# One layer-2 step in split halves, one step placed ahead of the next block, and residual additions by transfers, in an attention, LayerNorm, MLP and gate kernel

## The chip, the core and the metric

The kernel runs on one core of a Trainium2 chip. Its engines each run their own queue of instructions in a fixed order: TensorE (PE) multiplies matrices into PSUM, ScalarE (ACT), VectorE (DVE) and GpSimd (POOL) work elementwise, SyncE (SP) issues most transfers (DMAs). An engine that needs what another makes waits on a semaphore, and what stands behind the waiting instruction in its queue waits too. The metric is the device time of one execution in microseconds, as a median of several runs; lower is better.

## The reference

Three stages follow one another: a mutual attention between 8 batches of 512 tokens and 32 state tokens, a normalised MLP with a residual, and a gated output. Cut to what is computed:

```python
scores = scale * x @ state.T            # per batch and head, 8 heads of 64
xread = softmax(scores) @ state         # [8, 8, 512, 64]
sread = softmax(scale * state @ x.T) @ x  # [8, 8, 32, 64]
x = concat([xread, sread], axis=2)      # -> [8, 576, 512]
xn = (x - mean) / sqrt(var + 1e-6) * g_ln
x = x + relu(xn @ w_ch1) @ w_ch2        # 512 -> 2048 -> 512
gate = sigmoid(causal_conv5(x, conv_w))
out = (gate * (x @ w_val)) @ w_out
```

## The kernel before

**Work and its tiles.** The tokens are cut into nine blocks: b = 0 to 7 are the 512 tokens of one batch each, block 8 holds the 256 state tokens. Everything lies with the model or hidden columns on the 128 partitions and the tokens along the free side, so one matmul is 128x128 by 128x512. `segment(b, f0, f1, ...)` runs the MLP of a block in steps f = 0 to 15 of 128 hidden columns. A step has three parts: layer 1 puts h into a PSUM tile (two buffers, named mm in the trace); the evacuation makes hid from it; layer 2 (`second`) adds hid times a slice of w2 to four PSUM accumulators, acc0 to acc3. Layer 2 of a step is put off by one: `run_pending` writes it behind the layer 1 of the next step, so the evacuation of h runs beside matmuls.

**Two kinds of products.** Most products are in split halves: a value is kept as a high and a low half in the fast float format, and `mm3` (L77 to L80) does three matmuls for one product. Block 0's steps 0 to 3 (`plain`, QF = 4) use plain float matmuls, in layer 1 (L729) and in layer 2 (L785); a plain matmul needs the high part alone. A step in split halves has six layer-1 matmuls (L734) and twelve for layer 2. For it ScalarE makes the high half of hid with a Relu (L763) and VectorE the low half (L770); both read h. Weights come in 512 KB loads; ScalarE (L573, L575) and VectorE (L581, L583, L585, custom instructions) decode them, and for split steps ScalarE makes the high half (L653, or L631 for those that were first used plain) and VectorE the low one (L654, L634). The slots of this decode are handed out by `weights`.

**Blocks 0 and 1 are interleaved:** steps 0 to 7 of block 0, steps 0 to 7 of block 1, steps 8 to 15 of block 0, steps 8 to 15 of block 1; then blocks 2 to 7, block 8, and the value, gate and output stage. At the end of each of these half passes `second` scales each accumulator by the row of 1/std on VectorE (L799, into a t tile) and adds it to the block's residual x (L802). After a block's last step x goes to DRAM (x2d) and its last four columns are copied (the halo) for the convolution.

**m groups.** The first layer's weights are combined with the attention's state beforehand: `m_group` (L147) multiplies them into two PSUM tiles, `m_evac` (L158) scales and shifts them into mb, and `split_sb` (L73, L74) splits mb in halves of m. A group m (b, q) feeds four steps of layer 1. The groups for (0, 1) and (1, 0) are made in the middle of block 0's first pass. Group (0, 1) takes its two PSUM tiles from the mm buffers of h, group (1, 0) from the at buffers, in which the attention scores of block 1 stand before. The scores are centred and squared around L474, L476, L478 and L482 (LayerNorm of the attention's result), their row maxima are the reduces of L284, and ScalarE's exp (L286) reads them.

**What sets the order.** PE's order is the order in which the code is written. The orders of ACT, DVE, POOL and SP come from a scheduler that goes by priorities: `at_prio` sets one, HLEAD = 4000 puts work on PE's path ahead, DLEAD = 3000 the decode, and `behind` ties an instruction behind a marked one.

## Time and profile before

| | us |
|---|---|
| median of 3 runs (870.91 to 871.29) | 871.06 |
| the profiled execution, in all | 870.83 |
| its span in the trace | 868.9 |
| PE busy | 862.1 |
| DVE busy | 587.7 |
| ACT busy | 369.7 |
| POOL busy | 199.4 |

The span is what the trace shows from the first to the last instruction; about 2 us lie around it. Busy times are those of the profiled execution. In the page's groups PE's largest lines are the three products of layer 2 (L78 to L80, 560 each, 211 to 213 us) and layer 1 (L734, 744, 194.2 us). PE's total of waits is read in the view of waits, and what the other engines do beside it in the timelines, where each row gives its start from the span's start, its length and, in brackets, the idle time ahead of it and what ended it.

### The profile page before, as it was taken

How to read it: one execution, taken by the hardware profiler on the slowest of the kernel's cores; microseconds unless marked ns; L12 is line 12 of the kernel's file. 1: busy time of each engine (PE TensorE's matmuls, PEld its weight loads, DVE VectorE, ACT ScalarE, POOL GpSimd, SP SyncE). 2: the span in 40 equal slices, each digit the busy share in tenths (PEclk: the TensorE clock that was granted, in tenths of full speed). 3: DMA queues.
4: the chain of work that ended last, by engine and by line, in shares of the span. 5: the costliest groups of instructions: out<-in, count | busy, mean ns of one | idle time of the engine just before them, and what ended most of it. 6: DMA issues, size and time to landing. Idle time of an engine off the chain costs nothing.

```text
span 868.9 us, 12589 instructions
## 1 busy us (share of the span) xinstructions
PE 862.1 (99%) x4941; PEld 661.2 (76%) x4942; DVE 587.7 (68%) x995; ACT 369.7 (43%) x696; POOL 199.4 (23%) x162
## 2 busy tenths in 40 slices
PE   9999999999999999999999999999999999999998
PEld 3367767677777777778777777777899888888886
DVE  6999983874746754563674566353389799988870
ACT  5965942233333332432332343132256465455432
POOL 0020200013135133312513422252201223322100
PEclk9999999999999999999999999999999999999999
DMA  9925200321312221230231103010140212223212
GB/s 360 406 85 154 95 29 0 123 79 51 100 53 77 81 72 42 69 99 19 76 98 52 49 11 67 1 49 1 51 144 2 98 73 97 73 98 97 91 55 73
DMA packets 35643, 72.80 MB, mean 84 GB/s; under 512 B 11904, under 2 KB 20608, under 8 KB 31488
## 3 DMA queue, kind: packets, MB, share of 16 engines
q1 hardware_dynamic: 34816, 71.60, 23.9%
q8 instruction: 39, 0.64, 0.3%
q10 hardware_dynamic: 768, 0.40, 0.2%
q14 instruction: 20, 0.16, 0.1%
HBM read 51.01 MB, written 20.97 MB: 83 GB/s over the span
## 4 chain that ended last, share of the span: by engine, by line
PE 86%; DVE 3%; ACT 1%; DMA 0%; issue 0%; DVEq 0%; ACTq 0%
PE mm L734 18%; PE acc L78 16%; PE acc L79 16%; PE acc L80 16%; PE mm L80 2%; PE mm L78 2%; PE mm L79 2%; PE at L80 2%; PE at L78 2%; PE at L79 2%; PE at L147 2%; PE mm L147 1%; PE at L337 1%; PE acc L397 1%; DVE mb L158 1%; PE at L221 1%
## 5 line engine op out<-in xcount | busy, mean ns | idle before, releaser
L78 PE MATMUL acc<-hid,w 128*128 128x512 f32 (+1 forms) x560 | 212.6, 380 | 0.4 <-DVE x L402 0.2
L79 PE MATMUL acc<-hid,w 128*128 128x512 f32 (+1 forms) x560 | 211.4, 378 | 0.0
L80 PE MATMUL acc<-hid,w 128*128 128x512 f32 (+1 forms) x560 | 211.4, 378 | 0.0
L770 DVE SCALAR_TENSOR_TENSOR hid<-mm,hid 128x512 fp32r<-128x512 f32 (+1 forms) x140 | 91.6, 654 | 156.5 <-ACT hid L763 156.3
L734 PE MATMUL mm<-ahl,m 128*128 128x512 f32 x744 | 194.2, 396 | 0.5
L763 ACT ACTIVATE hid<-mm 128x512 fp32r<-128x512 f32 (+2 forms) x144 | 82.3, 571 | 215.5 <-PE mm L734 196.4
L734 PEld LDWEIGHTS mm<-ahl,m 128*128 128x128 f32 x744 | 137.0, 188 | 47.6 <-DVE mb L158 9.3
L78 PEld LDWEIGHTS acc<-hid,w 128*128 128x128 f32 x560 | 105.3, 188 | 24.7 <-issue 1.7
L80 PEld LDWEIGHTS acc<-hid,w 128*128 128x128 f32 x560 | 105.4, 188 | 20.0
L79 PEld LDWEIGHTS acc<-hid,w 128*128 128x128 f32 x560 | 105.4, 188 | 19.1
L861 DVE SCALAR_TENSOR_TENSOR ahl<-big,cw,ahl 128x511 f32<-128x511 f32 (+3 forms) x128 | 102.1, 843 | 0.3
L74 POOL TENSOR_TENSOR m<-mb,m 128x512 fp32r<-128x512 f32 x50 | 65.0, 1320 | 111.1 <-ACT m L73 111.0
L73 ACT ACTIVATE m<-mb 128x512 fp32r<-128x512 f32 x62 | 39.0, 632 | 80.8 <-DVE mb L158 80.5
L847 POOL TENSOR_TENSOR w<-big,w 128x512 fp32r<-128x512 f32 x24 | 37.9, 1611 | 93.0 <-ACT w L845 93.0
L79 PE MATMUL acc<-w,raw 128*128 128x512 f32 (+1 forms) x144 | 54.3, 377 | 0.0
L80 PE MATMUL acc<-w,raw 128*128 128x512 f32 (+1 forms) x144 | 54.3, 377 | 0.0
L78 PE MATMUL acc<-w,raw 128*128 128x512 f32 (+1 forms) x144 | 54.3, 377 | 0.0
L387 POOL TENSOR_TENSOR rstd<-rstd,nhalf 128x16 f32<-128x16 f32 (+1 forms) x9 | 25.7, 2854 | 114.3 <-DVE rstd L385 114.2
L799 DVE TENSOR_TENSOR t<-acc,t 128x512 f32<-128x512 f32 (+1 forms) x44 | 27.8, 660 | 24.3 <-PE acc L80 24.3
L802 POOL TENSOR_TENSOR x<-t,x 128x512 f32<-128x512 f32 x20 | 25.1, 1287 | 78.7 <-DVE t L799 78.7
L873 ACT ACTIVATE ahl<-ahl 128x512 f32<-128x512 f32 (+1 forms) x36 | 21.6, 608 | 45.6 <-DVE ahl L861 45.3
L902 DVE TENSOR_TENSOR w<-ahl,w 128x512 fp32r<-128x512 f32 (+1 forms) x36 | 30.7, 859 | 13.0 <-ACT w L901 12.8
(202 smaller groups left out, 1258.8 us busy)
## 6 DMA issues: line engine op xcount, KB each, us to landing
w<-in_w SPq DMA_DIRECT2D x20, 512.0 KB, 8.0
big<-in_xT SPq DMA_DIRECT2D x8, 1024.0 KB, 4.9
big<-in_xk SPq DMA_DIRECT2D x8, 1024.0 KB, 5.2
x2d<-x SPq DMA_DIRECT2D x8, 1024.0 KB, 4.2
big<-x2d SPq DMA_DIRECT2D x8, 1024.0 KB, 4.8
out<-hid SPq DMA_DIRECT2D x16, 512.0 KB, 2.8
raw<-in_w SPq DMA_DIRECT2D x12, 512.0 KB, 5.6
a2d<-t SPq DMA_DIRECT2D x48, 64.0 KB, 1.7
```

What stands on the lines that cost most here:

```text
L73: a = nc.scalar.activation(hi, src, AF.Copy)
L74: eng.tensor_tensor(lo, src, hi.bitcast(F32), op=ALU.subtract)
L78: nc.tensor.matmul(acc, lhsT=wh, rhs=xl, start=first, stop=False)
L79: nc.tensor.matmul(acc, lhsT=wl, rhs=xh, start=False, stop=False)
L80: nc.tensor.matmul(acc, lhsT=wh, rhs=xh, start=False, stop=last)
L734: nc.tensor.matmul(h, lhsT=m[:, u, w, cols], rhs=ahls[b][:, u, x], start=(i, u) == (0, 0), stop=(i, u) == (2, 1),)
L763: a = nc.scalar.activation(hid[:, 0], h, AF.Relu)
L770: marks["dve"] = nc.vector.scalar_tensor_tensor(hid[:, 1], h, 0.0, hid[:, 0].bitcast(F32), op0=ALU.max, op1=ALU.subtract)
L799: marks["dve"] = nc.vector.tensor_tensor(t, accs[d], rrow, op=ALU.mult)
L847: nc.gpsimd.tensor_tensor(lo, src, hi.bitcast(F32), op=ALU.subtract)
L861: t = nc.vector.scalar_tensor_tensor(g[:, j:], x[:, :n - j], cw_sb[:, k, PAD - j:TAPS - j], g[:, j:], op0=ALU.mult, op1=ALU.add)
L902: a = nc.vector.tensor_tensor(hl[:, 1], gt[:, e], hl[:, 0].bitcast(F32), op=ALU.subtract)
```

## The change

Four things are changed. Line numbers behind the change are larger by 4 to 14 (L147 is then L151, L463 and L459 of before are L467 and L463, L78 to L80 are L81, L734 is L747, L763 is L777, L770 is L784, L785 is L799, L799 is L813, L585 is L589).

1. Step 3 of block 0 does its layer 2 in split halves (`plain_out`): twelve matmuls of L81 in place of four plain ones, the high by high product first. VectorE makes a low half of its hid (L784), and w2_3 is split right after its decode (`split_last`, L73 and L74), where before it was split later with the other three.
2. Block 0's eighth step (f = 7) writes its layer 2 ahead of block 1's first layer 1 (`run_pending` at (1, 0, 0)), where before it stood behind it.
3. For group (0, 1) the m group, its sum and its evacuation are written ahead of `weights`, where before `weights` came first; the low halves of some w2 splits are tied behind the group's low half.
4. In the four half passes of blocks 0 and 1, the sixteen additions of VectorE at L802 become sixteen transfers that POOL issues and that add t to x where it lies (L817, 128x512, 256 KB each). L813 writes t tiles from the same six buffers as before, and the x2d store and the halo copy read the same x.

```diff
+    def mm3(acc, wh, wl, xh, xl, first, last, low_last=False):
+        terms = [(wh, xl), (wl, xh), (wh, xh)]
+        if low_last:
+            terms.reverse()
+        for i, (w, x) in enumerate(terms):
+            nc.tensor.matmul(acc, lhsT=w, rhs=x, start=first and i == 0, stop=last and i == 2)
...
+    def plain_out(b, f):
+        return b == 0 and f < QF - 1
...
-            return lambda: decode_a(r, c), add, lambda: None
+
+            def split_last():
+                w2s[j] = hl = sb([P, 2, DM], F32R, f"w2_{j}")
+                split_sb(hl[:, 0], hl[:, 1], c, nc.vector)
+
+            return lambda: decode_a(r, c), add, split_last if j == QF - 1 else lambda: None
...
             if j < QF + 2:
                 behind(hi, "parts")
+                behind(lo, "group_low")
...
+            if (b, f, f0) == (1, 0, 0):
+                at_prio(base + 200)
+                run_pending()
             at_prio(base)
             h = ps(ps_mm, "mm", [P, n])
...
                     colsum_parts(1)
+                    m_group(*unit, "mm")
+                    colsum(1)
+                    m_evac(*unit)
                     weights(base)
                     at_prio(base - 1500)
-                    m_group(*unit, "mm")
-                    colsum(1)
                 else:
                     m_group(*unit)
-                m_evac(*unit)
+                    m_evac(*unit)
...
-            if not plain(b, f):
+            if not plain_out(b, f):
                 marks["dve"] = nc.vector.scalar_tensor_tensor(
...
-                        eng.tensor_tensor(dst, grouped(b, t), grouped(b, x1[:, d, :]), op=ALU.add)
+                        if b < 2:
+                            nc.gpsimd.dma_start(out=dst, in_=t, accum_op=ALU.add)
+                        else:
+                            eng.tensor_tensor(dst, grouped(b, t), grouped(b, x1[:, d, :]), op=ALU.add)
...
-    order = order[:12] + [("s", j) for j in range(QF)] + order[12:]
+    order = order[:12] + [("s", j) for j in range(QF - 1)] + order[12:]
```

**At the m group (0, 1).** PE before, from layer 1 of step 3 (mm_415) over the colsum matmuls to the two halves of the group (mm_443, mm_444), with the engines that each instruction waits for:

```order
L729 MATMUL mm_415<-aT_288,m_307 128x512 x2
L182 MATMUL at_418<-w_2_70_330,g_82 32x512 [waits DVE_49,Activation_49]
L182 MATMUL at_418<-w_2_70_330,g_82 32x512 [waits DVE_49]
L182 MATMUL at_418<-w_3_88_390,g_82 32x512 [waits DVE_49] x2
L147 MATMUL mm_443<-w_2_70_330,stg_224 32x512 [waits Activation_49]
L147 MATMUL mm_443<-w_2_70_330,stg_224 32x512
L147 MATMUL mm_443<-w_3_88_390,stg_224 32x512 x2
L147 MATMUL mm_444<-w_2_70_330,stg_224 32x512 [waits Activation_49]
```

PE after, the same place (mm_418 is step 3's h, mm_428 and mm_429 the group's halves):

```order
L742 MATMUL mm_418<-aT_288,m_307 128x512 x2
L186 MATMUL at_421<-w_2_70_330,g_82 32x512 [waits DVE_49,Activation_49]
L186 MATMUL at_421<-w_2_70_330,g_82 32x512 [waits DVE_49]
L186 MATMUL at_421<-w_3_88_390,g_82 32x512 [waits DVE_49] x2
L151 MATMUL mm_428<-w_2_70_330,stg_224 32x512 [waits Activation_49]
L151 MATMUL mm_428<-w_2_70_330,stg_224 32x512
L151 MATMUL mm_428<-w_3_88_390,stg_224 32x512 x2
L151 MATMUL mm_429<-w_2_70_330,stg_224 32x512 [waits DVE_49]
```

The rows stand in the same order, but the group's second half, which takes the buffer of step 3's h, waits for Activation before and for DVE now. DVE before, from the decode of w2_3 (w_14_76) on (c_425 and c_434 are w2_4 and w2_5):

```order
L585 ISA w_14_76_350<-w_3_24_123,w_14_76_350 128x1024
L581 TENSOR_SCALAR w_3_88_390<-w_3_88_390 128x512
L583 TENSOR_SCALAR w_3_88_390<-w_3_88_390 128x512
L585 ISA w_3_88_390<-w_13_25_125,w_3_88_390 128x1024
L581 TENSOR_SCALAR c_425<-c_425 128x512
L263 TENSOR_TENSOR ahl_471<-aT_288,ahl_471 128x512 x2
L581 TENSOR_SCALAR c_434<-c_434 128x512
L583 TENSOR_SCALAR c_425<-c_425 128x512
L583 TENSOR_SCALAR c_434<-c_434 128x512
L585 ISA c_425<-w_4_28_131,c_425 128x1024
L585 ISA c_434<-w_5_29_133,c_434 128x1024
L654 TENSOR_TENSOR w_4_95_426<-c_425,w_4_95_426 128x512
```

DVE after, from the decode of w2_3 on (c_450 and c_459 are w2_4 and w2_5, hid_468 is step 3's hid):

```order
L589 ISA w_14_76_350<-w_3_24_123,w_14_76_350 128x1024
L74 TENSOR_TENSOR w_3_89_401<-w_14_76_350,w_3_89_401 128x512
L585 TENSOR_SCALAR w_3_88_390<-w_3_88_390 128x512
L587 TENSOR_SCALAR w_3_88_390<-w_3_88_390 128x512
L589 ISA w_3_88_390<-w_13_25_125,w_3_88_390 128x1024
L585 TENSOR_SCALAR c_450<-c_450 128x512
L267 TENSOR_TENSOR ahl_475<-aT_288,ahl_475 128x512 x2
L585 TENSOR_SCALAR c_459<-c_459 128x512
L587 TENSOR_SCALAR c_450<-c_450 128x512
L587 TENSOR_SCALAR c_459<-c_459 128x512
L589 ISA c_450<-w_4_28_131,c_450 128x1024
L784 SCALAR_TENSOR_TENSOR hid_468<-mm_418,hid_468 128x512
```

The low half of w2_3 (L74 w_3) is new behind its decode, and step 3's low half (L784 hid_468) stands between the two decodes of w2_4 and w2_5.

**Between the centring and the score maxima.** DVE before, from the last L474 to the two maxima of block 1's scores (at_534, at_535):

```order
L474 TENSOR_TENSOR t_110_493<-x_73_341,at_476 128x512
L585 ISA c_511<-w_7_31_137,c_511 128x1024
L654 TENSOR_TENSOR w_6_114_503<-c_502,w_6_114_503 128x512
L770 SCALAR_TENSOR_TENSOR hid_527<-mm_520,hid_527 128x512
L478 TENSOR_TENSOR t_107_483<-t_107_483,t_108_486 128x512
L478 TENSOR_TENSOR t_109_490<-t_109_490,t_110_493 128x512
L654 TENSOR_TENSOR w_7_116_512<-c_511,w_7_116_512 128x512
L482 TENSOR_TENSOR t_107_483<-t_107_483,t_109_490 128x512
L225 STREAM_TRANSPOSE t_121_544<-at_534 128x512
L225 STREAM_TRANSPOSE t_122_546<-at_535 128x512
L284 TENSOR_REDUCE nmax_550<-at_534 128x1
L284 TENSOR_REDUCE nmax_550<-at_535 128x1
```

DVE after, from the first step behind the four centrings (L478) on:

```order
L585 TENSOR_SCALAR c_506<-c_506 128x512
L585 TENSOR_SCALAR c_515<-c_515 128x512
L784 SCALAR_TENSOR_TENSOR hid_531<-mm_524,hid_531 128x512
L482 TENSOR_TENSOR t_108_487<-t_108_487,t_109_490 128x512
L587 TENSOR_SCALAR c_506<-c_506 128x512
L587 TENSOR_SCALAR c_515<-c_515 128x512
L482 TENSOR_TENSOR t_110_494<-t_110_494,t_111_497 128x512
L589 ISA c_506<-w_6_30_135,c_506 128x1024
L589 ISA c_515<-w_7_31_137,c_515 128x1024
L486 TENSOR_TENSOR t_108_487<-t_108_487,t_110_494 128x512
L663 TENSOR_TENSOR w_6_115_507<-c_506,w_6_115_507 128x512
L663 TENSOR_TENSOR w_7_117_516<-c_515,w_7_117_516 128x512
```

Behind these follow L784 hid_584, the two transposes and the two maxima (L288). The four tensor_scalars and one more decode of w2_6 and w2_7 (c_506, c_515) now stand in this piece, and a second low half of hid.

**At the end of block 0's first pass.** PE before, from layer 1 of (1, 0) (mm_742) to the first two of step 7's twelve (hid_675):

```order
L734 MATMUL mm_742<-ahl_641,m_614 128x512 [waits Activation_49] x2
L734 MATMUL mm_742<-ahl_641,m_614 128x512 [waits Pool_49] x2
L734 MATMUL mm_742<-ahl_641,m_614 128x512 [waits DVE_49] x2
L78 MATMUL acc_79_366<-hid_675,w_7_116_512 128x512
L79 MATMUL acc_79_366<-hid_675,w_7_116_512 128x512
```

Ten more of the twelve follow. PE before, from the last of them to the two tiles of L459 (mm_779 and mm_780, the state's product for block 1):

```order
L80 MATMUL acc_82_372<-hid_675,w_7_116_512 128x512
L459 MATMUL mm_779<-aT_638,sn_raw_113 64x512 [waits DMAHW4_49]
L459 MATMUL mm_779<-aT_638,sn_raw_113 64x512
L459 MATMUL mm_780<-aT_638,sn_raw_113 64x512 [waits DVE_49]
L459 MATMUL mm_780<-aT_638,sn_raw_113 64x512
```

The second tile waits for DVE's reading of mm_742, which has had the twelve matmuls to end.
PE after, from the last of step 7 on (mm_780 is now layer 1 of (1, 0), mm_791 and mm_792 the two tiles of L463):

```order
L81 MATMUL acc_82_372<-hid_687,w_7_117_516 128x512 x3
L747 MATMUL mm_780<-ahl_653,m_626 128x512 [waits Activation_49] x2
L747 MATMUL mm_780<-ahl_653,m_626 128x512 [waits Pool_49] x2
L747 MATMUL mm_780<-ahl_653,m_626 128x512 [waits DVE_49] x2
L463 MATMUL mm_791<-aT_650,sn_raw_113 64x512 [waits DMAHW4_49]
L463 MATMUL mm_791<-aT_650,sn_raw_113 64x512
L463 MATMUL mm_792<-aT_650,sn_raw_113 64x512 [waits DVE_49]
L463 MATMUL mm_792<-aT_650,sn_raw_113 64x512
```

Layer 1 of (1, 0) now stands directly ahead of L463, and the second tile's first matmul takes the buffer that DVE's low half of (1, 0) must have read; before, step 7's twelve matmuls stood between the two.

## Rows read from the trace of the kernel before

**Rows 1.** The page: busy us of each engine; PE's granted clock by slice.

```profile
PE 862.1 (99%) x4941; PEld 661.2 (76%) x4942; DVE 587.7 (68%) x995; ACT 369.7 (43%) x696; POOL 199.4 (23%) x162
...
PEclk9999999999999999999999999999999999999999
```

**Rows 2.** PE's waits: engine, line, releaser; us in total, times, longest.

```profile
PE mm L1095 <- DVE m L1090: 1.3, 1, 1.3
PE acc L221 <- DMA big<-in_xT: 0.6, 1, 0.6
PE acc L169 <- ACT cs L211: 0.2, 1, 0.2
PE acc L78 <- DVE x L402: 0.2, 1, 0.2
```

**Rows 3.** PE's timeline: start, us, engine, line, operation, tiles, count, idle time before.

```profile
39.14 1.09 PE L147 MATMUL mm<-w,stg 64*32 64x512 f32 x16
...
45.95 1.55 PE L734 MATMUL mm<-ahl,m 128*128 128x512 f32 x6
47.34 3.60 PE L785 MATMUL acc<-hid,w 128*128 128x512 f32 x8
50.86 1.09 PE L221 MATMUL at<-big,st_raw 64*32 64x512 f32 x16
...
53.37 0.39 PE L78 MATMUL acc<-hid,w 128*128 128x512 f32 x1
...
56.09 1.52 PE L734 MATMUL mm<-ahl,m 128*128 128x512 f32 x6
57.55 1.09 PE L147 MATMUL at<-w,stg 64*32 64x512 f32 x16
...
68.01 1.65 PE L734 MATMUL mm<-ahl,m 128*128 128x512 f32 x6
69.50 0.39 PE L78 MATMUL acc<-hid,w 128*128 128x512 f32 x1
...
72.31 1.09 PE L459 MATMUL mm<-aT,sn_raw 32*64 32x512 f32 x8
...
197.45 0.50 PE L78 MATMUL acc<-hid,w 128*128 128x512 f32 x1 [0.18 <-DVE x L402]
```

**Rows 4.** ACT's timeline, 33 to 70 us.

```profile
33.70 0.62 ACT L763 ACTIVATE hid<-mm 128x512 f32<-128x512 f32 x1
34.19 0.69 ACT L573 ACTIVATE w<-w 128x512 f32<-128x512 f32 x1
...
56.13 0.69 ACT L286 ACTIVATE t<-at,nmax 128x512 f32<-128x512 f32 x1
...
69.76 0.60 ACT L763 ACTIVATE hid<-mm 128x512 fp32r<-128x512 f32 x1 [1.09 <-PE mm L734]
```

**Rows 5.** DVE's timeline, 33 to 56 us.

```profile
33.83 0.69 DVE L585 CUSTOM_DVE_ANT_0 w<-w,w 128x1024 uint16<-128x1024 uint16 x1
34.91 0.43 DVE L581 TENSOR_SCALAR w<-w 128x512 f32<-128x512 f32 x1 [0.40 <-ACT w L573]
...
39.08 1.28 DVE L585 CUSTOM_DVE_ANT_0 c<-w,c 128x1024 uint16<-128x1024 uint16 x2
...
46.41 2.47 DVE L474 TENSOR_TENSOR t<-x,at 128x512 f32<-128x512 f32 x4
...
53.02 1.30 DVE L225 STREAM_TRANSPOSE t<-at 128x512 f32<-128x512 f32 x2
54.25 1.25 DVE L284 TENSOR_REDUCE nmax<-at 128x1 f32<-128x512 f32 x2
```

**Rows 6.** Transfers by kind: issuing queue, count, KB each, median us to landing.

```profile
raw<-in_w SPq DMA_DIRECT2D x12, 512.0 KB, 5.6
...
t<-a2d SPq DMA_DIRECT2D x12, 256.0 KB, 2.7
...
x1d<-t SPq DMA_DIRECT2D x32, 16.0 KB, 3.8
```

More of the change, by code (lines that the diff above doesn't have):

```diff
@@ L73, in split_sb @@
         a = nc.scalar.activation(hi, src, AF.Copy)
-        eng.tensor_tensor(lo, src, hi.bitcast(F32), op=ALU.subtract)
-        return a
-    def mm3(acc, wh, wl, xh, xl, first, last):
-        nc.tensor.matmul(acc, lhsT=wh, rhs=xl, start=first, stop=False)
-        nc.tensor.matmul(acc, lhsT=wl, rhs=xh, start=False, stop=False)
-        nc.tensor.matmul(acc, lhsT=wh, rhs=xh, start=False, stop=last)
+        return a, eng.tensor_tensor(lo, src, hi.bitcast(F32), op=ALU.subtract)
+    def mm3(acc, wh, wl, xh, xl, first, last, low_last=False):
[4 more added lines that the diff above has]
+            nc.tensor.matmul(acc, lhsT=w, rhs=x, start=first and i == 0, stop=last and i == 2)
     def at_prio(p):
@@ L162, in m_evac @@
             if not plain(b, 4 * q):
-                marks["group"] = split_sb(m[:, u, 0], m[:, u, 1], mb, nc.vector if b < 2 and (b, q) != (1, 0) else nc.gpsimd)
+                marks["group"], marks["group_low"] = split_sb(m[:, u, 0], m[:, u, 1], mb, nc.vector if b < 2 and (b, q) != (1, 0) else nc.gpsimd)
     def m_first(diag):
@@ L653, in split @@
             hi = nc.scalar.activation(hl[:, 0], c, AF.Copy)
-            nc.vector.tensor_tensor(hl[:, 1], c, hl[:, 0].bitcast(F32), op=ALU.subtract)
+            lo = nc.vector.tensor_tensor(hl[:, 1], c, hl[:, 0].bitcast(F32), op=ALU.subtract)
             if j < QF + 2:
                 behind(hi, "parts")
+                behind(lo, "group_low")
         mark = "group" if j == QF + 3 else "act"
@@ L761, in segment @@
             at_prio(base - HLEAD)
-            hid = sb([P, 2, n], F32 if plain(b, f) else F32R, "hid")
+            hid = sb([P, 2, n], F32 if plain_out(b, f) else F32R, "hid")
             a = nc.scalar.activation(hid[:, 0], h, AF.Relu)
@@ L783, in second @@
                     cols = slice(d * P, (d + 1) * P)
-                    if plain(b, f):
+                    if plain_out(b, f):
                         nc.tensor.matmul(accs[d], lhsT=plain_w2[f][:, cols], rhs=hid[:, 0], start=f == f0, stop=f == f1 - 1)
                     else:
-                        mm3(accs[d], w2s[f][:, 0, cols], w2s[f][:, 1, cols], hid[:, 0], hid[:, 1], f == f0, f == f1 - 1)
+                        mm3(accs[d], w2s[f][:, 0, cols], w2s[f][:, 1, cols], hid[:, 0], hid[:, 1], f == f0, f == f1 - 1, (b, f) == (0, QF - 1))
                     if f == f1 - 1:
```

## The prediction

> **What bounds the kernel now.** I read the page's busy shares first [rows 1]. TensorE (PE) is busy 862.1 of 868.9 us, and its granted clock shows 9, the top digit, in every slice, so it runs at its upper level, 2.4 GHz, from start to end. Its own waits come next [rows 2]: 1.3 us at the start, then 0.6, 0.2 and 0.2. So the time is PE's queue of matmuls almost without a gap. A matmul that goes away is worth its length, and a wait that the change opens on PE is added in full. The question is therefore not what VectorE (DVE) is spared, but whether PE, in its fixed order, now comes to places where the other engines are late. For that I read the first 80 us of PE, ScalarE (ACT) and DVE side by side [rows 3 to 5]: there DVE works almost back to back while PE never waits.
>
> Neighbouring instructions overlap a little in the timeline, so I count from start to start. Four of DVE's L474 take 2.47 us together where one shows some 0.68, so one costs 0.60 and the overlap is 0.08; a tensor_scalar of 0.43 costs 0.34 [rows 5].
>
> **Part 1, step 3 of block 0 in split halves: -0.8 us.** Before, the layer 2 of step 3 is the eight passes of L785 from 47.34 to 50.86, 3.52 us; a step in split halves is the twelve of L78 to L80 from 53.37 to 56.09, 2.72 us [rows 3]. The difference, 0.80 us, is PE work that is gone. Both stretches stand without waits, so I take it whole.
>
> **Part 1 also adds work ahead of step 3: a wait at the m group (0,1), +2.2 us.** ScalarE and VectorE now split w2_3 before block 0's step 2 is evacuated, and VectorE owes a low half of step 3's hid. PE's second half of the m group at L147 takes the PSUM buffer of step 3's h; before it waited for ACT's evacuation alone, now for DVE's low half (the order of PE below the change shows the wait turn from Activation to DVE). On DVE that low half stands behind the first of the two c decodes. Step by step:
> - Before, ACT starts to evacuate step 2 at 33.70, at once behind L463 [rows 4]. Now the high half of w2_3 stands between, and it needs DVE's L585 of that weight, which runs from 33.83 to 34.52 [rows 5]. So it starts near 34.6, takes 0.55 to its successor, as L573 at 34.19 does, and the evacuation starts at 35.15 instead of 33.70: ACT is 1.45 later.
> - ACT's next, L573 at 34.19, feeds DVE's L581 at 34.91, on which DVE already waited 0.40 [rows 5]. Now it starts at 36.36; DVE's new 0.60 (the low half of w2_3) falls into that wait.
> - From 34.91 to the end of the first c decode (the second of L585 starts 39.08 + 0.60 = 39.68) DVE has 4.77 us of back-to-back work [rows 5]: 41.13. The low half takes 0.68: 41.81; with 0.1 for the signal PE goes on at 41.9.
> - Without a wait PE would start that half at 39.14 plus half of L147's 1.09 less the overlap, 0.51: 39.65 [rows 3]. Wait: 2.2.
>
> The bounds: if ACT's delay were swallowed and only DVE's own 0.60 counted, the half would start at 41.05, a wait of 1.4; with a few signals of 0.1 more on the way, 2.4. I take 2.2, since the 0.40 of waiting on ACT shows that DVE stands on ACT's rhythm there.
>
> **The new order of `weights` and m_group: a wait at the m group (1,0), +2.2 us.** The mb and m halves now go ahead of the weights, and the four decode steps of w2_6 and w2_7 stand behind the four L474. Count DVE from the first L474 to the end of the second score reduce (L284). Before: 46.41 to 54.25 + 1.25 = 55.50, 9.1 us, of which 48.81 (46.41 + 4 times 0.60) to 53.02, 4.2 us, is other work between L474 and the transposes [rows 5]. Now that other work is nine full instructions and four tensor_scalars, 6.8 us. In all, seventeen of 0.60 and four of 0.34: 11.6 us. ACT's exps follow. In before, the second starts 56.13 and ends 56.82, when PE comes to L147 at 57.55 [rows 3, 4]: 0.73 us of cover. From PE's L734 of (0,4), at 45.95, DVE's first L474 stands 0.46 later. The reduces therefore end 12.1 after that mark, and the second exp some 1.6 later (two short nmax, two exps), at 13.7. PE's way from the mark is 1.39 + 2.72 (step 3, now split) + 2.51 + 2.72 + 1.46 = 10.80 to L147, and 0.51 more to its second half, which takes the second score's buffer: 11.3, with a margin for a signal 11.4 [rows 3]. So 2.2 to 2.3; I take 2.2. Two causes add: 2.5 from DVE and 0.8 that PE is now faster, less the cover of 0.73 and some 0.3 of rounding. Bounds: 1.5, if DVE's delay after the first wait leaves it ahead of PE by the 0.46 and the exps pipeline with the reduces as before; 2.6, if each step carries its signal.
>
> **Part 2, step 7's layer 2 ahead of block 1's first layer 1: +1.2 us.** It adds no instruction. Before, PE ran L734 of (1,0) from 68.01, then the twelve of step 7 from 69.50, then L459 at 72.31 [rows 3]: the 2.72 us of step 7 hid the evacuation of (1,0). Now L734 of (1,0) is followed at once by L459, whose second half takes the buffer of (1,0)'s h and waits for DVE's low half. Evacuation by the rows: matmuls end at 69.50, ACT starts 69.76 and ends 70.36 [rows 4], DVE's low half 0.68 and a signal 0.1: 1.7 us after the end of layer 1. The first half of L459 covers 0.5 of it. Wait: 1.2; bounds 1.1 and 1.8 (if one DVE instruction of 0.6 is in its way). What the move gives in return, an earlier end of block 0's accumulators, PE does not wait for here [rows 2].
>
> **Part 3, residual additions by transfers: -0.3 us.** Sixteen DVE additions of 0.60, 9.6 us of DVE, go. Almost none of it stood on PE's path: of PE's waits only the 0.2 at L78, at 197.45, ends on DVE work that such additions stand ahead of: 0.18 of wait and 0.11 in its first matmul, 0.50 instead of 0.39 [rows 2, 3]. I give back 0.3, and up to 0.5 if the 0.2 at L169 goes with it.
>
> The transfers: four of 256 KB per pass, issued by GpSimd (POOL), each reading t and the target and writing the sum. Behind them wait: x2d's store and the halo copy, with much time; and DVE's fourth L799, since its t takes the first's buffer. On DVE behind that stand the mb of (1,1) and all that PE needs next. By the rows the first t is there about 1.4 us after step 7's end, the issue can go at 1.5, and the fourth must start by about 9.0, where before DVE came to it with the mb still in time: the transfer has about 7 us. The trace has no transfer that POOL issues and none that accumulates. The nearest rows: 256 KB from DRAM 2.7 us, 512 KB of raw weights 5.6, 16 KB x1d stores 3.8 [rows 6]. An accumulating one moves t, the old and the new value, three times 256 KB, so I place it between the 2.7 and some 8 (three times 2.7); the nearest by size is the 5.6. Up to 7 it costs 0 on the path, and I take 0; a gain below that I have already counted. Above 7 each us costs about one us in block 0, so 8 would add 1.0. POOL has room for the issues (199.4 of 868.9 busy, [rows 1]).
>
> The rows have no price for a transfer of GpSimd's own. The Trainium skill, "DMA: Bandwidth & Descriptors", section "Anatomy of one DMA — SWDGE (gpsimd) path", gives one of about 2.0 us plus the bytes over 436 KB per us; by that page it is an estimate of 2.6 us here, and the sum would stay +4.5.
>
> **The sum.** -0.8 + 2.2 + 2.2 + 1.2 - 0.3 = +4.5 us. On the profiled run, 868.9 of span and 870.83 in all, that is 875.3; the median of the runs, 871.06, is 0.23 above it, and from it I forecast 875.6. With all bounds low: -0.8 + 1.4 + 1.5 + 1.1 - 0.5 = +2.7, 873.8; all high: -0.8 + 2.4 + 2.6 + 1.8 - 0.0 + 1.0 = +7.0, 878.1. That is the likeliest's own range.
>
> **The rivals.**
> - *Slow transfers.* The accumulating transfers take 10 us or more, held up while DVE works. For: from 46.41 to 55.50 DVE works without a gap [rows 5], and it is little freer where block 0's first pass ends. Against: the rows of plain transfers, at most 5.6 [rows 6]. It decides at 7 us; at 10 the fourth L799 comes 3 us late: 875.6 + 3 = 878.6; at 15, 883.6. The Trainium skill, "SBUF — State Buffer", section "Who interferes with whom", states that GpSimd's descriptors can't be written while VectorE runs one of its two-port operations; no run here shows it yet. Chance 0.17.
> - *The waits are mostly hidden.* If DVE ran the reordered chain in the old 9.1 us from L474 to the reduces instead of 11.6, which it would where the added steps fall into gaps of its own, the second wait is nil; if the third's low half also comes while L459's first half runs and the first is at its low bound, +1.4 - 0.8 - 0.3 + about 1: 872.4, within 0.2% (1.7 us). No wait at all gives 870.0, also within. Against: DVE has no such waits after 46.41 [rows 5]. Chance 0.12.
> - *Faster.* DVE's 9.6 us end waits elsewhere. It decides from PE waits of more than 1.7 us net: with all three new waits nil and every listed wait but the start's gone, -0.8 - 0.3 - 0.6 - 0.2 = -1.9, 869.2 us (chance 0.05). PE's rows hold no more [rows 2].
> - *The first wait or the second alone* is nil, since a chain is shorter than I count: about +2.3, 873.4. It lies in the range; it has 0.16, the forecast 0.50.
>
> **How the numbers follow.** 0.2% is 1.7 us, about what a measurement of this kernel can tell from no change. Faster 0.05, within 0.12 and a little of the forecast's lower edge, 0.13; slower the rest, 0.82. The range goes from 873.0, under the case with one wait nil, to 880.0, which takes in transfers of up to some 11 us; it leaves out the hidden case, the fast one and the slowest transfers, about 2 in 10.
>
> **What would show it.** In the changed kernel's PE waits: about 2.2 at the m group's L151 (before L147) on mm, behind DVE's hid; about 2.2 at L151 on at, behind ACT's t; about 1.2 at L463 (before L459) behind DVE's hid; step 3's layer 2 as twelve matmuls in 2.7 us; no wait behind L402 near 200. The issue-to-landing time of the new transfers decides part 3: under 7 us I am right, above I am wrong upward. If PE's waits stay under 1 us in all, the chains that I summed on DVE are the error; if a new wait near 200 or 330 us shows, the transfers are.

## The result

| | median us | runs, us | granted clock of the runs |
|---|---|---|---|
| before | 871.09 | 870.91 to 871.51 | 0.999 to 1.000 (in the runs beside the experiments) |
| after | 880.67 | 878.83 to 882.13 | 0.992 to 0.998 |

The changed kernel is slower: 1.0111 times the time before (95% interval 1.0097 to 1.0125). The forecast was 875.6 with a range of 873.0 to 880.0: the direction was right, the loss of 9.6 us is twice the forecast's 4.5, and the time lies above the range. The profiled execution took 880.45 us, 9.62 more than the one of before. Beside the size there is a second sign: the five runs differ by 3.3 us, where the runs of before lie within 0.6, and the slower runs have the lower granted clock.

The page after, its busy times:

```profile
PE 868.2 (99%) x4945; PEld 664.2 (76%) x4946; DVE 581.1 (66%) x980; ACT 369.7 (42%) x696; POOL 215.1 (24%) x178
```

PE is busy 6.1 us longer than in [rows 1], although its matmuls are cheaper by 0.7 us: some of them ran longer. PE's waits, in the columns of [rows 2]:

```profile
PE at L151 <- ACT t L290: 1.8, 1, 1.8
PE mm L151 <- DVE hid L784: 1.6, 1, 1.6
...
PE mm L747 <- ACT m L73: 0.4, 1, 0.4
PE mm L463 <- DVE hid L784: 0.4, 1, 0.4
```

Three new waits stand where the forecast put them, and one more of 0.4 us, L747 behind ACT's m. They are shorter than forecast (1.6, 1.8 and 0.4 for 2.2, 2.2 and 1.2): at the m group (0,1) and at L463 the half that runs alone fills 1.06 us of PE, where the forecast counted half of the pair's 1.02. The loss is therefore read from start to start below. PE's timeline at these places, to be read against [rows 3]:

```profile
39.51 1.06 PE L151 MATMUL mm<-w,stg 64*32 64x512 f32 x8
42.16 1.06 PE L151 MATMUL mm<-w,stg 64*32 64x512 f32 x8 [1.59 <-DVE hid L784]
43.16 1.12 PE L202 MATMUL at<-t,part 128*128 128x512 f32 x2
...
50.31 2.88 PE L81 MATMUL acc<-hid,w 128*128 128x512 f32 x12
53.13 1.09 PE L225 MATMUL at<-big,st_raw 64*32 64x512 f32 x16
...
58.38 1.52 PE L747 MATMUL mm<-ahl,m 128*128 128x512 f32 x6
61.73 2.60 PE L151 MATMUL at<-w,stg 64*32 64x512 f32 x16 [1.84 <-ACT t L290]
64.27 5.07 PE L81 MATMUL acc<-hid,w 128*128 128x512 f32 x12
69.17 0.63 PE L366 MATMUL mm<-t,ones 128*128 128x512 f32 x2
...
80.04 1.07 PE L463 MATMUL mm<-aT,sn_raw 32*64 32x512 f32 x4
81.52 1.07 PE L463 MATMUL mm<-aT,sn_raw 32*64 32x512 f32 x4 [0.41 <-DVE hid L784]
82.53 1.09 PE L151 MATMUL at<-w,stg 64*32 64x512 f32 x16
```

Rows of before at the same places that [rows 3] leaves out:

```profile
40.16 1.12 PE L198 MATMUL at<-t,part 128*128 128x512 f32 x2
...
58.56 0.50 PE L78 MATMUL acc<-hid,w 128*128 128x512 f32 x1
...
61.43 0.63 PE L362 MATMUL mm<-t,ones 128*128 128x512 f32 x2
```

And the granted clock in stretches of 2 us (start and end, length, busy us of PE, PEld, DVE, ACT and POOL with their instructions, PEclk, share of the DMA engines, GB/s):

```profile
60.00:62.00 2.00, 0.27 (x4) 0.15 (x8) 2.00 (x5) 1.87 (x6) 0.00 (x0) 0.97 0.00 0
62.00:64.00 2.00, 2.00 (x16) 0.20 (x8) 2.00 (x5) 1.16 (x4) 0.00 (x0) 0.50 0.00 0
...
68.00:70.00 2.00, 2.00 (x11) 1.58 (x10) 0.16 (x1) 0.00 (x0) 0.00 (x0) 0.82 0.00 0
```

PE stood still from 59.9 to 61.73, and from about 61.9 until about 68.7 us its granted clock was 0.50, the lower level, 1.2 GHz. The twelve matmuls of L81 at 64.27 took 4.90 us to the next row, where the same twelve of before took 2.87 (58.56 to 61.43). The page can't tell this: its forty digits of PEclk are all 9 after the change too, as in [rows 1], since a slice is 22 us long and averages a fall of 7 us away. In stretches of 5 to 100 us the trace of before shows 1.00 throughout its first 200 us.

**Where the 9.62 us are.** From start to start of the rows, after less before:

| place | after | before | difference |
|---|---|---|---|
| m group (0,1) | 39.51 to 43.16 | 39.14 to 40.16 | +2.63 |
| step 3's layer 2 | 50.31 to 53.13 | 47.34 to 50.86 | -0.70 |
| layer 1 and m group (1,0) | 58.38 to 64.27 | 56.09 to 58.56 | +3.42 |
| the twelve behind it | 64.27 to 69.17 | 58.56 to 61.43 | +2.03 |
| L463, first pair | 80.04 to 82.53 | 72.31 to 73.33 | +1.47 |
| L463, second pair | 87.85 to 89.39 | 78.65 to 79.67 | +0.52 |
| m group and layer 1 near 118 and 122 | 1.58 and 2.29 | 1.02 and 1.71 | +1.14 |
| attention (L401, before L397) and layer 2 near 204 | 1.14 and 2.80 | 1.74 and 3.23 | -1.03 |

That is +9.5 of the 9.8 by which the spans differ (878.7 and 868.9); the rest is the m group's later start (39.51 for 39.14) and small differences. The clock's part of the 3.42 and 2.03 is read from e1 below, which runs the group and the twelve behind it at full clock: 4.51 us (61.58 to 66.09) where this kernel takes 7.44 (61.73 to 69.17), so the fall costs 2.9. Without it the changed kernel would take an estimated 871.1 + 9.5 - 2.9 = 877.7.

### The profile page after: what moved, and what is told of

It reads as the page before. It is cut to its first block, busy times and chain, and to the rows that moved or that the text cites. A ratio compares the mean times of both kernels' runs of the same rounds, so it can differ in the third digit from the quotient of the medians.

```text
span 878.7 us, 12633 instructions
## 1 busy us (share of the span) xinstructions
PE 868.2 (99%) x4945; PEld 664.2 (76%) x4946; DVE 581.1 (66%) x980; ACT 369.7 (42%) x696; POOL 215.1 (24%) x178
## 4 chain that ended last, share of the span: by engine, by line
PE 84%; DVE 4%; ACT 1%; issue 0%; DMA 0%; SPq 0%
PE acc L81 48%; PE mm L747 18%; PE mm L81 8%; PE at L81 5%; PE at L151 1%; PE mm L151 1%; DVE mb L162 1%; PE acc L401 1%; PE at L341 1%; PE at L225 1%; DVE w L589 1%; DMA raw<-in_w 0%; DVE hid L784 0%; DVE t L250 0%; PE mm L384 0%
## 5 line engine op out<-in xcount | busy, mean ns | idle before, releaser
L81 PE MATMUL acc<-hid,w 128*128 128x512 f32 (+1 forms) x1692 | 390.3, 380 | 0.1
L81 PEld LDWEIGHTS acc<-hid,w 128*128 128x128 f32 x1692 | 305.9, 189 | 65.1 <-DVE r L298 1.7
L784 DVE SCALAR_TENSOR_TENSOR hid<-mm,hid 128x512 fp32r<-128x512 f32 (+1 forms) x141 | 92.4, 655 | 164.5 <-ACT hid L777 164.4
L747 PE MATMUL mm<-ahl,m 128*128 128x512 f32 x744 | 194.0, 396 | 1.0 <-ACT m L73 0.4
L777 ACT ACTIVATE hid<-mm 128x512 fp32r<-128x512 f32 (+2 forms) x144 | 82.2, 571 | 220.0 <-PE mm L747 200.9
L747 PEld LDWEIGHTS mm<-ahl,m 128*128 128x128 f32 x744 | 137.1, 188 | 48.0 <-DVE mb L162 9.3
L81 PE MATMUL acc<-w,raw 128*128 128x512 f32 (+1 forms) x432 | 94.1, 377 | 0.0
L81 PEld LDWEIGHTS acc<-w,raw 128*128 128x128 f32 x432 | 77.9, 188 | 15.1
L74 POOL TENSOR_TENSOR m<-mb,m 128x512 fp32r<-128x512 f32 x50 | 64.9, 1326 | 94.9 <-ACT m L73 94.9
L73 ACT ACTIVATE m<-mb 128x512 fp32r<-128x512 f32 x62 | 39.2, 632 | 85.6 <-DVE mb L162 85.1
L81 PE MATMUL at<-w,w 128*128 128x512 f32 (+1 forms) x216 | 51.0, 385 | 0.0
L81 PE MATMUL mm<-w,w 128*128 128x512 f32 (+1 forms) x204 | 48.1, 385 | 0.0
L81 PEld LDWEIGHTS at<-w,w 128*128 128x128 f32 x216 | 39.8, 188 | 8.2
L813 DVE TENSOR_TENSOR t<-acc,t 128x512 f32<-128x512 f32 (+1 forms) x44 | 27.6, 661 | 26.0 <-PE acc L81 23.5
L81 PEld LDWEIGHTS mm<-w,w 128*128 128x128 f32 x204 | 37.7, 188 | 7.9
L162 DVE SCALAR_TENSOR_TENSOR mb<-cs,sbn,at 128x512 f32<-128x512 f32 x40 | 28.5, 739 | 7.7 <-PE at L151 6.9
```

The costliest lines, as they stand in the source:

```text
L73: a = nc.scalar.activation(hi, src, AF.Copy)
L74: return a, eng.tensor_tensor(lo, src, hi.bitcast(F32), op=ALU.subtract)
L81: nc.tensor.matmul(acc, lhsT=w, rhs=x, start=first and i == 0, stop=last and i == 2)
L162: a = nc.vector.scalar_tensor_tensor(mb, cs[:, q], sbn[:, u], mp[u], op0=ALU.mult, op1=ALU.add)
L747: nc.tensor.matmul(h, lhsT=m[:, u, w, cols], rhs=ahls[b][:, u, x], start=(i, u) == (0, 0), stop=(i, u) == (2, 1),)
L777: a = nc.scalar.activation(hid[:, 0], h, AF.Relu)
```

## The experiments

The theory, called the pause theory: the three waits are the forecast's, and what was missed is that a pause of PE can be followed by several microseconds at half the clock. Its rivals: the clock falls for another reason (the transfers, DVE's load, or by itself); the transfers are the loss.

**e1: the second pause filled.** (The tile of zeros and its filling are left out here, and in e7 and e10.)

```diff
             if unit == (1, 0) and f % QF == 2:
                 at_prio(base - 1500)
+                for i in range(8):
+                    nc.tensor.matmul(accs[i % KT], lhsT=zeros[:, :P], rhs=zeros, start=False, stop=False)
                 m_steps(*unit)
```

> The changed kernel with eight more matmuls of zeros by zeros (bf16, 128x512, added into the accumulators, which stay as they are) in PE's queue directly ahead of the m group (1,0) at L151, where PE paused 1.84 us. Pause theory: the granted clock halved after 62 us because PE stood still there; with some 1.8 us of work in the pause the clock stays at 1.00, the m group and the twelve matmuls behind it lose no time, and 2.5 to 4 us come back: 876.5 to 878, granted clock 1.000. Rival (the clock falls for another reason, the transfers or the busy DVE): the clock still shows 0.992 to 0.998 and the time stays at 880 to 882.

Measured: 879.23 us median (877.91 to 879.6), clock 0.996 to 0.999. The profiled run, 877.91, is 2.5 less than that of after. PE's timeline there and the clock of the two stretches that were at 0.50 in after:

```profile
59.59 1.90 PE L772 MATMUL acc<-zeros 128*128 128x512 bf16 x8
61.58 1.73 PE L152 MATMUL at<-w,stg 64*32 64x512 f32 x16
63.24 3.02 PE L82 MATMUL acc<-hid,w 128*128 128x512 f32 x12
66.09 0.63 PE L367 MATMUL mm<-t,ones 128*128 128x512 f32 x2
```

```profile
62.00:64.00 2.00, 2.00 (x19) 0.83 (x12) 2.00 (x5) 1.16 (x4) 0.00 (x0) 1.00 0.00 0
64.00:66.00 2.00, 2.00 (x10) 1.63 (x9) 2.00 (x5) 1.54 (x3) 0.93 (x1) 1.00 0.00 0
```

More work in PE's queue, and the time falls: the eight take the pause's place, the group and the twelve run at full clock (2.85 us to the next row instead of 4.90 for the twelve). The group still takes 1.66 us for the 1.02 of before, since its second half starts late, behind the second exp. The profiled run is in the expected range; the median is not, since in the other runs the clock still fell somewhere (0.996 to 0.998). This kernel still has the pause of 1.6 us near 40, which e10 takes up.

**e2: VectorE's additions back.**

```diff
-                        if b < 2:
-                            nc.gpsimd.dma_start(out=dst, in_=t, accum_op=ALU.add)
-                        else:
-                            eng.tensor_tensor(dst, grouped(b, t), grouped(b, x1[:, d, :]), op=ALU.add)
+                        eng.tensor_tensor(dst, grouped(b, t), grouped(b, x1[:, d, :]), op=ALU.add)
```

> The changed kernel with VectorE's sixteen residual additions back in place of the transfers. Pause theory: the transfers hardly matter; the three waits of 1.84, 1.59 and 0.41 and the clock's fall stay, the late fourth L813 goes (-0.5 and up to -1.1 later) and the waits near 195 us come back (+0.95): 879.5 to 881.5. Rival (slow transfers are the loss): the time falls by 4 or more, to 876.5 or less.

Measured: 881.55 us (876.75 to 883.85), a ratio of 1.0105 (1.0083 to 1.0126), just above the expected 879.5 to 881.5, with no transfer of that kind in the kernel. So the transfers are not the loss. Its runs are the plainest view of the clock: 876.75 and 877.57 at 0.999, 881.33 to 881.79 at 0.993, 883.85 at 0.991. In the profiled run (881.79) the clock fell behind both pauses, which ended at 41.84 and at 64.77:

```profile
40.00:45.00 5.00, 3.42 (x14) 0.99 (x11) 2.39 (x5) 1.40 (x3) 0.00 (x0) 0.71 1.03 404
45.00:50.00 5.00, 5.00 (x8) 1.94 (x7) 3.67 (x6) 3.21 (x6) 0.00 (x0) 0.61 0.05 20
...
65.00:70.00 5.00, 5.00 (x25) 2.69 (x18) 4.93 (x11) 2.87 (x6) 1.74 (x2) 0.66 0.00 0
```

**e3: step 3 plain again.**

```diff
     def plain_out(b, f):
-        return b == 0 and f < QF - 1
+        return b == 0 and f < QF
...
-    order = order[:12] + [("s", j) for j in range(QF - 1)] + order[12:]
+    order = order[:12] + [("s", j) for j in range(QF)] + order[12:]
```

> The changed kernel with step 3 of block 0 plain again (four plain matmuls, no low half of hid, w2_3 split later); the order of the m group, step 7's place and the transfers stay. Pause theory: the wait at the m group (0,1) goes (-2.6), the step costs its 0.7 again, DVE is ahead by its two instructions and PE behind by 0.7, so the pause at the m group (1,0) shrinks to under 1 us and the clock doesn't fall: 873 to 875. Rival (the new order of the weights alone makes the second pause): pause and fall stay, 878 to 879.

Measured: 874.42 us (873.9 to 874.56), clock 0.998 to 1.000, as the pause theory says and 4 below its rival. PE's timeline has neither of the long pauses:

```profile
39.08 1.09 PE L151 MATMUL mm<-w,stg 64*32 64x512 f32 x16
...
57.62 2.02 PE L151 MATMUL at<-w,stg 64*32 64x512 f32 x16
59.57 3.02 PE L81 MATMUL acc<-hid,w 128*128 128x512 f32 x12
```

Its longest wait after the start is 1.0 us, near 103. The m group (0,1) at 39.08 runs in one piece again; at 57.62 the group (1,0) takes 1.95 to the next row instead of 1.02, a late second half and no standstill of microseconds. The split of step 3 is thus the condition of both long pauses: without it, the same order of the weights makes none.

**e4: the kernel before with the transfers alone** (the diff of e2 the other way round, on before).

> The kernel before with the sixteen residual additions by transfers and nothing else. Pause theory: first pass +0.5 to +1.5 (the third and fourth L813 wait for landings while loads run), near 195 us -0.9: 870.5 to 872.0, clock 1.000. Slow transfers: landings over 7 us hold DVE and then PE in the first pass, 874 or more. DVE relief: 869.5 or less.

Measured: 871.96 us (871.14 to 873.65, 11 runs), a ratio of 1.0007 (0.9998 to 1.0016). In the expected range. Here too the runs spread with the clock, 1.000 at 871.1 to 871.5 and 0.997 to 0.998 at 873.1 to 873.7; in the profiled run PE waited 0.41 us near 80 for DVE's mb, and a fall followed (0.50 from 82.1 to 85.6).

**e5: the m group (1,0) behind step 5's layer 2.**

```diff
-            if unit == (1, 0) and f % QF == 2:
-                at_prio(base - 1500)
-                m_steps(*unit)
...
             run_pending()
+            if unit == (1, 0) and f % QF == 2:
+                at_prio(base - 1500)
+                m_steps(*unit)
+                at_prio(base + 200)
```

> The changed kernel with the m group (1,0) written behind step 5's layer 2 instead of ahead of it, so PE comes to L151 2.7 us later and need not wait for the exps. Pause theory: the pause of 1.84 (2.4 with its split group) goes, and with it that place's clock fall: without falls 876.3 - 2.4 = 874, with a fall still possible at the first pause (42 us) up to 878; median 874 to 876. Rival (the clock falls without a pause): 878 or more with the fall still at 62 to 68 us.

Measured: 877.74 us (876.04 to 878.71), clock 0.995 to 0.998. The pause at the exps is gone, and no fall shows between 60 and 70; the profiled run fell at the first pause instead, from 42 to 49 us. The median lies above what was expected: PE now waits 0.24 and 0.68 at L308, and the clock fell in every run rather than in some.

**e6: step 7's layer 2 in its old place.**

```diff
-            if (b, f, f0) == (1, 0, 0):
-                at_prio(base + 200)
-                run_pending()
```

> The changed kernel without the new place of step 7's layer 2. Pause theory: L463's wait (1.47 from start to start) goes, perhaps with the x1d waits of the third L813 too (another 0.5): 1.5 to 2.0 less than the changed kernel at the same granted clock, so 878.5 to 880 with clock 0.992 to 0.998. Rival (the move pays by an earlier end of block 0's accumulators): same or slower than the changed kernel.

Measured: 877.92 us (876.45 to 883.49), less than the expected 878.5 to 880, which reckoned with a fall in every run. Three runs at clock 1.000 took 876.45 to 876.74, the other three, at 0.992 to 0.995, 879.11 to 883.49. L463 at 79.58 runs in 1.02 again, so the 1.47 is the move's; its second pair near 86 takes 1.89 instead of 1.54, so 0.35 goes back. The three clean runs give what the changed kernel's waits cost without any fall and without the move: 876.5 - 871.1 = 5.4 us.

**e7: a pause alone, in the kernel before.**

```diff
             if unit == (1, 0) and f % QF == 2:
                 at_prio(base - 1500)
+                for i in range(2):
+                    nc.tensor.matmul(accs[i], lhsT=zeros[:, :P], rhs=zeros, start=False, stop=False)
+                    for _ in range(2 * (1 - i)):
+                        nc.gpsimd.tensor_tensor(zeros, zeros, zeros, op=ALU.add)
                 m_steps(*unit)
```

> The kernel before with PE made to stand still once, ahead of the m group (1,0) near 57.5 us: a matmul of zeros, two POOL additions on the zeros that the next matmul of zeros must wait for, and that matmul; nothing else is changed. The two matmuls cost 0.45, the two additions (1.3 each by the POOL rows) about 2.6 to 2.9. Pause theory: the granted clock halves behind the pause in most runs, 0.992 to 0.998 over the run, and the time is 874.4 plus 2 to 6: 876 to 880, spread by 2 or more. Rival (the fall has another cause, such as the transfers or DVE's load): 874.0 to 874.8 with clock 1.000 and no spread.

Measured: 878.95 us (877.98 to 881.73), clock 0.992 to 0.998 in all five runs, with no split step, no transfer of the new kind and no new order. PE's two long waits in the profiled run:

```profile
PE acc L758 <- POOL zeros L760: 2.8, 1, 2.8
PE at L460 <- DVE mb L159: 2.0, 1, 2.0
```

The row of DVE behind the second wait:

```profile
79.69 1.29 DVE L804 TENSOR_TENSOR t<-acc,t 128x512 f32<-128x512 f32 x2 [3.18 <-DMA x1d<-t]
```

The clock:

```profile
58.00:61.00 3.00, 0.73 (x9) 0.28 (x17) 2.58 (x7) 0.95 (x2) 2.13 (x2) 1.00 0.00 0
...
80.00:85.00 5.00, 2.98 (x14) 1.43 (x14) 5.00 (x9) 2.81 (x6) 0.00 (x0) 1.00 0.28 105
85.00:90.00 5.00, 5.00 (x18) 3.34 (x13) 4.97 (x11) 3.17 (x7) 0.00 (x0) 0.66 0.34 117
```

The built pause of 2.8 us near 58 was followed by a second of 2.0 us near 82, behind DVE's mb, which came late because L804 (L799 of before) had stood 3.18 us for x1d stores. The clock held behind the first pause and fell behind the second. So neither the change's split step nor its transfers nor its order is needed for a fall, a wait of PE in the kernel before is enough, and a fall does not follow every pause. The expected 874.4 did not hold the second wait; with it the sum without a fall is 871.1 + 0.45 + 2.8 + 2.0 = 876.3, an estimate.

**e8: the transfers in the last half pass alone, on before.**

```diff
-                        eng.tensor_tensor(dst, grouped(b, t), grouped(b, x1[:, d, :]), op=ALU.add)
+                        if (b, f) == (1, NF - 1):
+                            nc.gpsimd.dma_start(out=dst, in_=t, accum_op=ALU.add)
+                        else:
+                            eng.tensor_tensor(dst, grouped(b, t), grouped(b, x1[:, d, :]), op=ALU.add)
```

> The kernel before with the residual additions of the last half pass alone (block 1, step 15) as transfers. Pause theory: the 0.95 near 193 to 197 us comes back and the first pass keeps its order: 870.2 to 870.7. Rival (transfers contend at that place too): 871.4 or more.

Measured: 870.37 us (870.0 to 871.04, 11 runs) beside 871.13 for before on that chip, a ratio of 0.9992 (0.9983 to 1.0000). As expected, and the one part of the change that shows a gain by itself, of 0.8 us, at the edge of its interval. PE's timeline near 193, first before, then here:

```profile
193.00 1.81 PE L397 MATMUL acc<-aT,sn_raw 32*64 32x512 f32 x16
194.74 0.40 PE L380 MATMUL mm<-parts,stack 128*128 128x16 f32 x2
```

```profile
193.31 1.21 PE L397 MATMUL acc<-aT,sn_raw 32*64 32x512 f32 x16
194.45 0.40 PE L380 MATMUL mm<-parts,stack 128*128 128x16 f32 x2
```

L397 takes 1.14 us to the next row, 1.74 before, and the gap of [rows 3] at L78 is gone.

**e9: the weights ahead of the m group again.**

```diff
-                behind(lo, "group_low")
...
                     colsum_parts(1)
+                    weights(base)
+                    at_prio(base - 1500)
                     m_group(*unit, "mm")
                     colsum(1)
-                    m_evac(*unit)
-                    weights(base)
-                    at_prio(base - 1500)
                 else:
                     m_group(*unit)
-                    m_evac(*unit)
+                m_evac(*unit)
```

> The changed kernel with the order of the weights and the m group as before (weights ahead of the m group, no tie of the low halves); all else stays. My step on the order: between the four centrings and the maxima DVE has eight instructions of 0.6 (4.8 us) instead of 6.8, so the pause at the m group (1,0) falls from 1.8 to under 1.2, while the one at the m group (0,1) stays at 1.6: 875.5 without a clock fall, 876 to 879 with one. Rival (the split of step 3 alone makes the second pause): 1.8 stays, 879 or more.

Measured: 877.8 us (876.48 to 879.32). The first pause stays at 1.6; the second shrinks from 1.84 to two of 0.16 and 0.18 us, and the time lies in the range expected with a fall. The profiled run has two falls, behind the first pause (43.4 to 46.8) and behind a wait of 0.47 at L463 (80.9 to 84.4). With e3, where the new order stands without the split and no long pause shows, both are needed for the second pause: the split that makes PE quicker and DVE busier, and the order that puts 2 us more of DVE's work ahead of the maxima.

**e10: both pauses filled.** e1, and ahead of the second half of the m group (0,1):

```diff
         for u in range(2):
+            if (b, q, u) == (0, 1, 1):
+                for i in range(10):
+                    nc.tensor.matmul(fill_accs[0][i % KT], lhsT=zeros[:, :P], rhs=zeros, start=False, stop=False)
             for p in range(KT):
```

> e1 with the first pause filled too: ten more matmuls of zeros between the two halves of the m group (0,1), 2.3 us where PE stood 1.6. Pause theory: with both long pauses worked through the clock stays at 1.000 in nearly every run: 877 to 878, all runs within 1 us. Rival (the clock falls by itself or by DVE's load): spread of 2 and more and clock down to 0.995 as in e1 (877.9 to 879.6) and the changed kernel (878.8 to 882.1).

Measured: clock 0.998 to 1.000 in all five runs, where e1 has 0.996 to 0.999 and after 0.992 to 0.998. Three runs took 877.81 to 877.97, as expected. Two took 880.25 and 880.77, which was not expected, and not by the clock: in the profiled one (880.25, clock 0.999) DVE stood 4.27 us ahead of the third L821 (L813 of after), and PE then waited 0.9 for it at L82. The DVE row, and the transfers issued from 70 to 90 us (queue, KB each, median us to landing):

```profile
84.28 0.69 DVE L821 TENSOR_TENSOR t<-acc,t 128x512 f32<-128x512 f32 x1 [4.27 <-DMA x1d<-t]
```

```profile
x<-t POOLq DMA_DIRECT2D x4, 256.0 KB, 6.3
...
x1d<-t SPq DMA_DIRECT2D x4, 16.0 KB, 6.8
```

The wait ends with the last of the four x1d stores (landed at 84.15), not with a new transfer: of these the first had landed at 83.12 and the second came at 84.86. How much of it the transfers cause is taken up in the next section.

**e11: another tile for the m group (0,1).**

```diff
-            at_ps([P, S]) if where == "at" else ...
+            at_ps([P, S]) if where == "at" or (b, q, u) == (0, 1, 1) else ...
```

> The changed kernel with the second PSUM tile of the m group (0,1) taken from the at buffers, which the colsum's tile leaves early, instead of the mm buffer that step 3's low half reads. Pause theory: the first pause (2.6 from start to start) goes, the one at the m group (1,0) stays with its clock falls: 874.4 without a fall, 875 to 878 with one. Rival (the low half was not what PE waited for): 879 or more, the wait at 40 us stays.

Measured: 878.88 us (878.09 to 880.0), clock 0.993 to 0.998. The first pause is gone, so the low half is what PE waited for. But the second one grew from 1.84:

```profile
PE at L151 <- ACT t L290: 3.1, 1, 3.1
```

PE comes to the m group (1,0) 2.9 us earlier (57.0 for 59.9), and the group starts only 1.6 earlier (60.15 for 61.73). Without a fall that would be about 877.7 - 1.6 = 876.1, an estimate, instead of the 874.4 expected, and the clock was low in every run. The two pauses are not independent, since DVE's chain sets the second.

**e12: what should be left without the waits.** e11's tile, e5's place of the group, e6's old place of step 7 and e8's transfers, in the changed kernel.

> What should be left of the change without its waits: step 3 split with e11's tile, the m group (1,0) behind step 5's layer 2 as in e5, step 7's layer 2 in its old place, transfers in the last half pass alone as in e8. Pause theory: -0.7 for step 3, -0.9 for the last half pass, up to +0.9 for the waits at the transposes (L308) that e5 showed: 869.5 to 871.0, clock 1.000. Rival (DVE's added low halves cost PE elsewhere): 872 or more.

Measured: 873.42 us (873.26 to 874.06), clock 0.999 to 1.000. No fall, no spread, and yet 2.0 over before, in the rival's range. Its waits of 0.3 to 0.7 us that before hasn't:

```profile
PE at L308 <- ACT t L312: 0.7, 1, 0.7
...
PE at L308 <- DVE mb L162: 0.4, 1, 0.4
PE mm L744 <- ACT m L73: 0.4, 1, 0.4
PE at L151 <- ACT t L290: 0.3, 1, 0.3
```

They add to 1.8, and some also separate two halves of a group that run beside each other otherwise. In PE's timeline this kernel takes 9.20 us from the layer 1 at 55.52 to the one at 64.72, before 6.60 (56.09 to 62.69). The two waits at L308 stand there, and e5, whose place of the group this kernel has, shows them too (0.24 and 0.68). It also keeps the new order of the weights. So e12 shows that taking out the long waits in this way leaves a loss; that the split of step 3 alone costs more than the 0.7 us that it spares PE is not shown.

**All traces together.** Apart from the last few microseconds, the granted clock falls twelve times in the fourteen profiled runs, and each fall begins within 2.3 us of the end of a wait of PE of 0.41 us or more. Four of the falls last 6.8 us and eight 3.4. All twelve follow a wait at an m group or at L463 (L459, L460), whose matmuls have tiles of 64*32 or 32*64 in the rows. The waits elsewhere, 1.00 us at L747 (e3), 0.85 at L82 (e10) and 0.68 at L308 (e5), were followed by none, nor was the built one of 2.76 (e7). Whether a fall takes the pause alone or also such matmuls beside it, no run separates.

## Why the prediction was wrong

- **Step 3's saving:** -0.8 forecast, -0.70 measured. Right.
- **The wait at the m group (0,1):** +2.2 forecast, 2.63 measured. The chain over ACT's split, the decode and the low half was right: DVE's low half started at 41.42, forecast 41.13, and PE's second half at 42.16, forecast 41.9. The term was small by 0.4: the halves of the group run side by side (1.02 us for both, [rows 3]), so once the second is late it takes 1.00 of its own, not 0.51. The row of DVE after:

```profile
41.42 0.68 DVE L784 SCALAR_TENSOR_TENSOR hid<-mm,hid 128x512 fp32r<-128x512 f32 x1
```

- **The wait at the m group (1,0):** +2.2 forecast; 1.89 of pause and, by e1's group at full clock, some 0.6 for the second half. DVE's chain from the four centrings to the end of the maxima took 11.64 us (49.14 to 60.78), forecast 11.6. Right in place and nearly in size, though the first half waited already. e9 bears out that the order of the weights makes the larger part; e3 that the split must be there too.
- **Step 7 ahead of layer 1:** +1.2 forecast, 1.47 measured: the second half started 1.48 us behind the first, 0.2 sooner than forecast, and took 1.0 of its own, not 0.5.
- **The additions:** -0.3 forecast, -1.0 measured. [rows 2] shows a gap of 0.2, but L397 stood late as well, 1.74 us where 1.14 do (e8), and no wait was listed for that. The listed waits of before were too small a base.
- **The transfers:** 0 forecast. They landed 3.5 to 7.3 us after the issue in the first pass, one of the four above the bound of 7, 3.3 to 4.6 in the second and third and 3.9 to 5.5 in the last. But the wrong transfer was looked at: the third L813 waits ahead of the fourth, for the x1d stores, one of whose t buffers it takes. The changed kernel's transfers issued from 76 to 90 us (queue, KB each, median us to landing), and then two rows of DVE's timeline there:

```profile
x<-t POOLq DMA_DIRECT2D x4, 256.0 KB, 6.0
...
x1d<-t SPq DMA_DIRECT2D x4, 16.0 KB, 5.4
```

```profile
84.79 0.69 DVE L813 TENSOR_TENSOR t<-acc,t 128x512 f32<-128x512 f32 x1 [2.38 <-DMA x1d<-t]
...
86.93 1.40 DVE L162 SCALAR_TENSOR_TENSOR mb<-cs,sbn,at 128x512 f32<-128x512 f32 x2
```

The x1d stores took 3.8 us in [rows 6] and 5.4 here. DVE stood 2.38 us, mb came late, and L463's second pair lost the 0.52. The transfers made the stores later by a part of that only. The first of the four stores lands 0.2 us behind a load issued ahead of it, with the transfers (83.29 behind 83.11 here) and without (74.97 behind 74.79 in before, 78.95 behind 78.75 in e7, where DVE stood 3.18). Where a new transfer is issued ahead of the third store (after, e1, e9 to e11), the last store lands 1.4 to 2.3 us behind the first, in the other traces 0.5 to 0.6. So some 0.8 us of the 2.38 here, and 1.7 of the 4.27 in e10, are an estimate of what the transfers do to the stores. Whether the third takes a buffer of these stores at all is not set by the transfers alone: in e2, where VectorE adds, it did not wait for them, in e7, where VectorE adds too, it did.

- **The clock: the step that failed.** The prediction's first paragraph reads from [rows 1] that PE's clock is at its upper level from start to end, and says that a wait which the change opens on PE is added in full; the sum then prices each new wait by its length. No term and no rival asked whether the clock of before would still hold in a kernel with waits of 2 us, though [rows 1, 2] are the trace of a kernel that has none after its start. What the runs showed in its place: behind the pause of 1.84 us the clock was at 0.50 for 6.8 us, which cost 2.9 us in the profiled run, and the loss differs from run to run. The waits and gains alone come to about +6.6, 877.7, within the likeliest's own range (873.8 to 878.1). They exceed the forecast's +4.5 by the late second halves above and by losses that no term held, 0.52 at L463's second pair and 1.1 near 118 and 122 us, less 0.7 that the additions gave back beyond the forecast.
- **The rival of slow transfers** gives 878 to 884 and would have held the number, by the wrong mechanism: e2 has no such transfer and is as slow.

Not settled: near 118 and 122 us PE loses 1.1 us (a late second half of an m group, and L747 behind ACT's m). The wait at L747 stands in e1, e6, e9 to e11 and, at 116, in e12, not in e2 to e5; none of the runs took it apart. Nor is settled why one pause is followed by a fall and another is not.

## What to carry to other kernels

A wait on an engine that never waits is not priced by its length alone: add what follows it at the lower clock, and expect a spread between runs. Two matmul groups that run beside each other cost twice when one of them is held, so count the late one in full. And before an engine is relieved or a transfer added, look for who takes the buffer next: the bound that counts is that of the first waiter, which need not be the transfer itself.
